# One strict load order on one queue, staged weights, and the first chunk's layers run ahead, in a fused attention and two-layer kernel

## The chip, the cores and the metric

One core of one Trainium2 chip. The metric is the device time of a whole execution in microseconds (us); lower is better. Each kernel has several executions. The ratios compare fast runs alone. The kernel before ran in every set on the same chip as the kernels that are compared with it.

## The reference

Eight batches of eight-head attention (576 positions, head size 64). The first four heads look at the last 32 positions ("local"), the other four at every 32nd ("strided"). The result, 4608 tokens of 512 features, goes through two dense layers.

```python
scores = scale * q @ k.T
scores = where(mask_local if h < 4 else mask_strided, scores, -1e9)
x = softmax(scores) @ v                  # to (4608 tokens, 512)
h = x @ w_in                             # 512 -> 2048
g = maximum(h, 0) + alpha * minimum(h, 0)
out = g @ w_out                          # 2048 -> 512
```

q, k, v and the weights arrive as float32. The kernel computes in float16.

## The kernel before

The tokens are cut into nine chunks of 512. Chunk n needs the attention of batches up to n (chunk 1 needs part of batch 1, and so on, since a batch is 576 tokens). Layer 1 of a chunk is 16 linear pieces of four matmuls of 512 columns, layer 2 the same, 0.86 us each at full clock. The attention is cut into some 30 pieces a batch: transposes of q and k ("tp"), scores ("sp") with their exp on ScalarE and mask, products with v ("pv") with their norms on DVE, transposes of the result ("xp"). The trick of the tuned kernel is to set these small pieces between linear ones, so that TensorE never waits for the other engines.

A steady loop does, for every n, layer 2 of chunk n and layer 1 of chunk n+1 beside the attention of batch n+2. What differs between the two kernels is the ramp in front of it, and the first turn (n = 1):

```python
# weights: gpsimd DMAs that cast to float16 on the way
def load_w(c, second): nc.gpsimd.dma_start(win16[...] or wout16[...], ...)
...
gate = cpool.tile([128, 16], F16)                      # SyncE waits for w_in here
nc.sync.dma_start(gate, win16[:, 0, 1008:1024])
...                                                    # then batch 1's loads
for m in range(16):                                    # layer 1, chunk 0
    lin1_piece(0, m, True)
    if m == 8: ...                                     # casts of batch 1, loads of batch 2, w_out
    attn_n(0 if m < 12 else 1, end1)
while pos["i"] < end1: attn_step(end1)                 # rest of batch 1, first pieces of batch 2
for m in range(16):                                    # layer 1, chunk 1
    lin1_piece(1, m, True)
    attn_n(0 if m < 8 else 1, end2)
for i in range(16):                                    # layer 2, chunk 0
    lin2_piece(0, i)
    attn_n(2, end2)
for n in range(1, NCH):                                # the full loop
    for i in range(16):
        lin2_piece(n, i);  attn_step(ab)
        lin1_piece(n + 1, i);  attn_step(ab)
```

The order of pieces above is the order of instructions on every engine, and a held instruction holds those behind it (in the changed kernel, scores that TensorE ends at 73.2 us get their exp at 79.05, behind an output copy that waits). Four `lin2_piece` calls end in one output copy ("osb") on ScalarE and one store on SyncE. In the traces that follow, line 437 of the kernel before is 454 of the changed one (layer 1), 482 is 499 (layer 2), 487 is 504 (output copy).

The softmax here doesn't subtract the row's maximum and nothing guards it: scores larger than these inputs give would overflow.

## Time and profile before

| | kernel before |
|---|---|
| median time | 363.43 us (363.37 to 363.66, 3 runs) |
| first linear piece | 32.2 us |
| TensorE full from | 119.1 us to the end |
| ramp: layer 1 chunk 0, layer 1 chunk 1, layer 2 chunk 0 start at | 32.2, 79.3, 97.6 us |
| one turn of the full loop | 34.5 us |

Read it so: from 119.1 us on the kernel is a steady loop with a full TensorE, and of this loop the change touches only the first turn, n = 1. All that the change can win or lose is the moment at which that loop begins. The lines that carry this are in the prediction below.

### The profile page before, as it was taken

The page shows a single profiled execution, that of the slowest core. Times are in us where ns is not written, and L with a number is a line of the kernel's source. Part 1 is how long each engine was busy: PE and PEld are TensorE (multiplying, and loading weights), DVE is VectorE, ACT ScalarE, POOL GpSimd, SP SyncE. Part 2 cuts the span into 40 slices and gives each one's busy share as a digit, 9 for nine tenths or more (in the row PEclk, how much of TensorE's full clock was granted, in tenths as well). Part 3 has the DMA queues.
Part 4 walks back from the last instruction along what each step waited for, and adds up shares of the span by engine and source line. Part 5 has one row for each costly group of instructions (what it writes and reads, how often), then busy time and mean ns, then how long its engine had stood idle before and what let it go on. Part 6 is the DMA issues. An engine that isn't in the chain of part 4 may idle for free.

```text
span 363.0 us, 6353 instructions
## 1 busy us (share of the span) xinstructions
PE 329.7 (91%) x2449; PEld 185.8 (51%) x2449; DVE 226.5 (62%) x423; ACT 177.6 (49%) x328; POOL 138.7 (38%) x170
## 2 busy tenths in 40 slices
PE   6658974649998999999999999999999999999996
PEld 3353443424564455555557776555555444444444
DVE  5776898837864477758676767585767444444410
ACT  2532663516643556565656565656554544444421
POOL 5360473381576365546455564556151000000000
PEclk9977997559999999999999999999999999999999
DMA  7989999999936083519352820000000010010012
GB/s 210 218 134 287 199 238 196 275 206 280 232 103 203 32 232 96 175 42 246 96 175 53 242 63 32 29 32 29 31 32 29 29 60 29 29 60 29 29 61 87
DMA packets 52926, 44.08 MB, mean 121 GB/s; under 512 B 33616, under 2 KB 38112, under 8 KB 52896
## 3 DMA queue, kind: packets, MB, share of 16 engines
q1 hardware_dynamic: 47712, 37.11, 38.8%
q0 software_dynamic: 4640, 5.51, 8.2%
q10 hardware_dynamic: 544, 1.05, 1.0%
q8 instruction: 19, 0.31, 0.4%
q14 instruction: 11, 0.09, 0.1%
HBM read 38.42 MB, written 9.44 MB: 132 GB/s over the span
## 4 chain that ended last, share of the span: by engine, by line
PE 81%; DMA 9%; DVE 3%; ACT 2%; POOL 2%; issue 2%; SPq 1%; POOLq 0%; ACTq 0%
PE hps L437 34%; PE ops L482 34%; DMA sttl<-in_k_dram 6%; PE sp L251 4%; PE tp L210 3%; PE pv L280 3%; DMA stv<-in_v_dram 3%; PE xp L297 2%; SPq L100 1%; PE ops L473 1%; DVE et L266 1%; DVE x L289 1%; ACT osb L487 1%; POOL vs L151 1%; ACT et L259 0%
## 5 line engine op out<-in xcount | busy, mean ns | idle before, releaser
L437 PE MATMUL hps<-xT,win 128*128 128x512 f16 (+1 forms) x640 | 148.3, 364 | 0.8 <-DVE gT L450 0.8
L450 DVE SCALAR_TENSOR_TENSOR gT<-neg,oma,hps 128x512 f16<-128x512 f32 x144 | 106.9, 743 | 59.2 <-ACT neg L447 56.7
L482 PE MATMUL ops<-wout,gT 128*128 128x512 f16 x560 | 141.4, 379 | 2.0 <-ACT osb L487 2.0
L447 ACT ACTIVATE neg<-hps 128x512 f32<-128x512 f32 x144 | 86.2, 599 | 94.9 <-PE hps L437 94.0
L266 POOL TENSOR_TENSOR et<-et,consts 128x384 f16<-128x384 f16 (+2 forms) x60 | 54.2, 908 | 85.4 <-ACT et L259 84.5
L437 PEld LDWEIGHTS <-win 128*128 128x128 f16 x640 | 60.1, 99 | 49.8 <-issue 6.0
L482 PEld LDWEIGHTS <-gT 128*128 128x128 f16 x560 | 50.4, 98 | 49.0 <-issue 2.8
L259 ACT ACTIVATE et<-sp 128x384 f16<-128x384 f32 (+2 forms) x96 | 45.6, 490 | 24.6 <-PE sp L251 24.4
L289 DVE TENSOR_TENSOR x<-pv,rc 72x384 f16<-72x384 f32 (+2 forms) x80 | 42.2, 527 | 2.7
L223 DVE COPY qpad<-tp 64x1024 f16<-64x1024 f16 x32 | 39.0, 1220 | 3.8 <-PE tp L210 3.5
L251 PE MATMUL sp<-qpad,kT 128*128 128x144 f16 (+1 forms) x224 | 32.8, 248 | 7.2 <-DVE qpad L240 3.8
L287 DVE RECIPROCAL rc<-pv 72x6 f32<-72x6 f32 (+2 forms) x80 | 14.8, 186 | 37.5 <-PE pv L280 37.3
L280 PEld LDWEIGHTS <-et 72*128 72x128 f16 (+1 forms) x448 | 25.6, 102 | 23.7 <-POOL et L262 3.7
L251 PEld LDWEIGHTS <-kT 128*128 128x128 f16 x224 | 20.5, 103 | 25.4 <-issue 5.7
L487 ACT COPY osb<-ops 128x512 f32<-128x512 f32 x35 | 20.5, 586 | 21.9 <-PE ops L482 21.9
L236 ACT COPY kT<-tp 128x1024 f16<-128x1024 f16 x16 | 16.2, 1011 | 20.0 <-PE tp L210 20.0
L280 PE MATMUL pv<-vl,et 128*128 128x65 f16 x192 | 12.4, 201 | 8.1 <-POOL et L262 3.4
L280 PE MATMUL pv<-vs,et 72*128 72x65 f16 x256 | 16.9, 200 | 1.7 <-DVE x L289 0.9
L151 POOL CAST vs<-stv 72x1024 f16<-72x1024 f32 x16 | 16.9, 1084 | 2.9 <-DMA stv<-in_v_dram 2.9
L297 PE MATMUL xp<-consts,x 72*128 72x72 f16 (+1 forms) x224 | 15.3, 211 | 2.0 <-DVE x L289 1.7
L297 PEld LDWEIGHTS <-x 72*128 72x128 f16 (+1 forms) x224 | 12.8, 104 | 7.2 <-DVE x L289 2.4
L151 POOL CAST tl<-sttl 128x512 f16<-128x512 f32 x8 | 4.9, 618 | 28.6 <-DMA sttl<-in_k_dram 28.6
(48 smaller groups left out, 186.4 us busy)
## 6 DMA issues: line engine op xcount, KB each, us to landing
out_dram<-osb SPq DMA_DIRECT2D x35, 256.0 KB, 2.0
stq<-in_q_dram SPq DMA_DIRECT2D x16, 512.0 KB, 6.7
stk<-in_k_dram SPq DMA_DIRECT2D x12, 512.0 KB, 5.0
stv<-in_v_dram SPq DMA_DIRECT2D x7, 768.0 KB
stv<-in_v_dram SPq DMA_DIRECT2D x8, 576.0 KB
win<-in_moe_w_in_dram POOLq DMA_DIRECT2D x4, 512.0 KB, 9.3
wout<-in_moe_w_out_dram POOLq DMA_DIRECT2D x4, 512.0 KB, 13.4
stk<-in_k_dram ACTq DMA_DIRECT2D x2, 512.0 KB, 8.4
```

The costliest lines, as they stand in the source:

```text
L151: keep(nc.gpsimd.tensor_copy(o, i))
L223: keep(nc.vector.tensor_copy(split(qpads[u % 2][rr, :, hh, :])[0], main[rr]))
L251: keep(nc.tensor.matmul(sp[:, 2 * w * x : 2 * w * x + 2 * w], P.kT[:, k0 : k0 + 128], P.qpad[:, :, w * t : w * t + w], start=(x == 0), sto ...
L259: keep(nc.scalar.activation(et[0:r, 0:n], sp[0:r, 0:n], AF.Exp, scale=SCALE))
L266: keep(eng.tensor_tensor(ev, ev, m.unsqueeze(1).to_broadcast([r, n // w, w]), op=ALU.mult))
L280: keep(nc.tensor.matmul(pv[:, 65 * x : 65 * x + 65], et[0:r, c : c + 128], v16[0:r, t, 2 * P.pr + hh, :], start=(x == 0), stop=(x == nb - ...
L289: keep(nc.vector.tensor_tensor(P.x16[0:w, c0 : c0 + 64 * nb].rearrange("r (c e) -> r c e", e=64), pvv[:, :, 0:64], rc[0:w, 0:nb].unsqueeze ...
L297: keep(nc.tensor.transpose(xp[:, P.w * t : P.w * t + P.w], P.x16[0 : P.w, 128 * t : 128 * t + 128], ident[0 : P.w, 0 : P.w]))
L437: keep(nc.tensor.matmul(hps[:, dst : dst + w], win16[:, kk, 128 * m : 128 * m + 128], xT[:, kk, src : src + w], start=(kk == 0 and x == 0) ...
L447: keep(nc.scalar.activation(neg, hps, AF.Relu, scale=-1.0))
L450: keep(nc.vector.scalar_tensor_tensor(gTs[n][:, m, :], neg, oma[:, m : m + 1], hps, op0=ALU.mult, op1=ALU.add))
L482: keep(nc.tensor.matmul(ops, gTs[n][:, kf, 128 * mt : 128 * mt + 128], wout16[:, kf, :], start=(kf == 0), stop=(kf == 15)))
```

## The change

The intent: TensorE idles in front because batch 1 arrives late, so order the loads by when they are needed, all on SyncE's queue: batch 0, w_in, w_out, batches 1 and 2. With w_out there early, layer 2 of chunk 0 need not come after layer 1 of chunk 1. Both layers of chunk 0 run right after batch 0's attention and cover batch 1's loads. The weights come as float32 into the v buffers and are cast on GpSimd. The core of the diff:

```diff
-    st = spool.tile([128, 2, 512], F32, tag="qk", bufs=6, ...)
+    st = spool.tile([128, 2, 512], F32, tag="qk", bufs=4, ...)
-                keep(nc.vector.tensor_copy(split(qpads[u % 2][rr, :, hh, :])[0], main[rr]))
+                copy = nc.scalar.copy if b < 3 and hh else nc.vector.tensor_copy
+                keep(copy(split(qpads[u % 2][rr, :, hh, :])[0], main[rr]))
-        eng = nc.vector if P.b < 2 else nc.gpsimd
+        eng = nc.vector if P.b < 2 and i % 2 == 0 else nc.gpsimd
...
     def load_w(c, second):
-        ... nc.gpsimd.dma_start(win16 / wout16, ...)
+        st = spool.tile([128, 2048], F32, tag="v", bufs=4, name="stw")
+        keep(nc.sync.dma_start(st.rearrange(...), w_ap(c, second)[0]))
+        staged[(c, second)] = st
+    def cast_w(c, second, eng0="pool", eng1="pool"): ...   # two copies to float16
...
+    for second in (False, True):
+        for c in range(4):
+            load_w(c, second)
+    for b in (1, 2):
+        load_qk(b, True); load_tail(b); load_v(b, True)
+        load_qk(b, False); load_v(b, False)
...
     for m in range(16):
         lin1_piece(0, m, True)
-        ...
-        attn_n(0 if m < 12 else 1, end1)
+        if m in (4, 7, 10, 13):
+            cast_w((m - 4) // 3, True, "pool", "pool" if m < 13 else "act")
+        attn_n(0, end1)
+    cast_qk(1, True, "dve", "act"); cast_tail(1, "pool"); cast_v(1, True)
+    for i in range(16):
+        lin2_piece(0, i)
+        attn_n(0 if i < 5 else 1, end1)
+        if i == 12:
+            cast_qk(1, False, "dve", "act"); cast_v(1, False)
     while pos["i"] < end1:
         attn_step(end1)
...
     for m in range(16):
         lin1_piece(1, m, True)
-        attn_n(0 if m < 8 else 1, end2)
-    for i in range(16):
-        lin2_piece(0, i)
-        attn_n(2, end2)
+        attn_n((0 if m < 2 else 1) if m < 8 else 2, end2)
     while pos["i"] < end2:
         attn_step(end2)
...
     for n in range(1, NCH):
         for i in range(16):
+            now = 0 if n == 1 and i < 3 else ab
```

Smaller parts: the attention of batches 0 to 2 becomes a sequence of its own for each batch (strided heads, then local), one more exp buffer, more v buffers.

More of the change, by code (lines that the diff above doesn't have):

```diff
@@ L82 @@
     xT = cpool.tile([128, 4, RING], F16)
-    NE = 8
+    NE = 9
     qpads = [cpool.tile([128, 2, 2, S], F16, name=f"qpad{i}") for i in range(2)]
@@ L97, in load_qk @@
         for nm, src, eng in (("q", q, nc.sync), ("k", k, k_eng or nc.sync)):
-            st = spool.tile([128, 2, 512], F32, tag="qk", bufs=6, name=f"st{nm}")
+            st = spool.tile([128, 2, 512], F32, tag="qk", bufs=4, name=f"st{nm}")
             base = src[b, h0 : h0 + 1, 0:1, :]
@@ L114, in load_v @@
     def load_v(b, strided):
-        st = spool.tile([128, 2048], F32, tag="v", name="stv")
+        st = spool.tile([128, 2048], F32, tag="v", bufs=4, name="stv")
         if strided:
@@ L324, in X, with first, sc, pv @@
         return lambda: x_piece(pairs[g])
-    feed(T(1, "q"), 0)
-    feed(T(1, "k"), 0)
-    for g in (2, 3):
-        for i in range(3):
-            feed(Sc(g, i), 0)
-    for g in (2, 3):
-        for i in range(3):
-            feed(Pv(g, i), 0)
-    feed(T(0, "q"), 0)
-    feed(T(0, "k"), 0)
-    feed(X(2), 0)
-    feed(X(3), 0)
-    for g in (0, 1):
-        for i in range(3):
-            feed(Sc(g, i), 0)
-    for g in (0, 1):
-        for i in range(2):
-            feed(Pv(g, i), 0)
-    feed(X(0), 0)
-    feed(X(1), 3)
+    def first(u0, u1):
+        A, Bp = (2 * u0, 2 * u0 + 1), (2 * u1, 2 * u1 + 1)
+        def sc(gs):
+            for g in gs:
+                for i in range(3):
+                    feed(Sc(g, i), -1)
+        def pv(gs):
+            for g in gs:
+                for i in range(len(pairs[g].pgroups)):
+                    feed(Pv(g, i), -1)
+        def tr(u):
+            feed(T(u, "q"), -1)
+            feed(T(u, "k"), -1)
+        def xs(gs, last=False):
+            for g in gs:
+                feed(X(g), g if last else -1)
+        tr(u0)
+        sc(A)
+        tr(u1)
+        sc(Bp[:1])
+        pv(A)
+        sc(Bp[1:])
+        xs(A)
+        pv(Bp)
+        xs(Bp)
+    first(1, 0)
     end0 = len(pieces)
+    first(3, 2)
+    end1 = len(pieces)
+    first(5, 4)
+    end2 = len(pieces)
     casts = []
@@ L354, in plan_casts @@
         u = (g + 3) // 2
-        if u >= 2 * B or u < 2:
+        if u >= 2 * B or u < 7:
             return []
@@ L359, in plan_casts @@
         return [(b, strided, nm, pr) for nm, pr in names]
-    for g in range(3, npair + 2):
+    for g in range(11, npair + 2):
         a, p, t, x = g, g - 1, g + 1, g - 2
-        okA = 4 <= a < npair
-        okP = 4 <= p < npair
-        okT = 4 <= t < npair and t % 2 == 0
-        okX = 4 <= x < npair
+        okA = 12 <= a < npair
+        okP = 12 <= p < npair
+        okT = 12 <= t < npair and t % 2 == 0
+        okX = 12 <= x < npair
         nP = len(pairs[p].pgroups) if okP else 0
@@ L488, in lin2_piece, with w_ap, cast_w @@
             keep(nc.sync.dma_start(out[r0 : r0 + 128, :], osb))
-    def load_w(c, second):
-        if second:
-            keep(nc.gpsimd.dma_start(
-                wout16[:, 4 * c : 4 * c + 4, :],
-                moe_w_out[512 * c : 512 * c + 512, :].rearrange("(kf p) c -> p kf c", p=128)))
-        else:
-            keep(nc.gpsimd.dma_start(
-                win16[:, :, 512 * c : 512 * c + 512],
-                moe_w_in[:, 512 * c : 512 * c + 512].rearrange("(kk p) c -> p kk c", p=128)))
+    staged = {}
+    def w_ap(c, second):
+        if second:
+            return (moe_w_out[512 * c : 512 * c + 512, :].rearrange("(kf p) c -> p kf c", p=128),
+                    wout16[:, 4 * c : 4 * c + 4, :])
+        return (moe_w_in[:, 512 * c : 512 * c + 512].rearrange("(kk p) c -> p kk c", p=128),
+                win16[:, :, 512 * c : 512 * c + 512])
+    def load_w(c, second):
+        st = spool.tile([128, 2048], F32, tag="v", bufs=4, name="stw")
+        keep(nc.sync.dma_start(st.rearrange("p (x c) -> p x c", x=4), w_ap(c, second)[0]))
+        staged[(c, second)] = st
+    def cast_w(c, second, eng0="pool", eng1="pool"):
+        s4 = staged[(c, second)].rearrange("p (x c) -> p x c", x=4)
+        dst = w_ap(c, second)[1]
+        cast_copy(eng0, dst[:, 0:2, :], s4[:, 0:2, :])
+        cast_copy(eng1, dst[:, 2:4, :], s4[:, 2:4, :])
     def warm(n):
@@ L520 @@
     load_v(0, False)
+    for second in (False, True):
+        for c in range(4):
+            load_w(c, second)
+    for b in (1, 2):
+        load_qk(b, True)
+        load_tail(b)
+        load_v(b, True)
+        load_qk(b, False)
+        load_v(b, False)
     for i in range(2):
@@ L525 @@
         keep(nc.vector.memset(kTs[i][:, :, 608:672], 0.0))
-    warm(12)
-    cast_part(0, True, "q", 0, "dve")
-    cast_part(0, True, "k", 0, "act")
-    cast_tail(0, "pool")
-    cast_part(0, True, "v", 0, "pool")
-    cast_part(0, True, "v", 1, "pool")
-    cast_part(0, False, "v", 0, "pool")
-    load_w(0, False)
-    cast_part(0, False, "v", 1, "pool")
-    load_w(1, False)
-    load_w(2, False)
-    load_w(3, False)
-    apt = pspool.tile([128, 512], F32, tag="ps", name="apt")
-    for i in range(end0):
-        if i == 8:
-            cast_part(0, False, "q", 0, "dve")
-            cast_part(0, False, "k", 0, "act")
-        attn_step(end0)
-        if i < 2:
-            warm(4)
-        elif i < 14:
-            warm(1)
-        if i == 13:
-            keep(nc.vector.tensor_copy(id16, ident[0:16, 0:16]))
-            keep(nc.tensor.transpose(apt[:, 0:16], alpha_r, id16))
-            keep(nc.vector.tensor_scalar(
-                oma, apt[:, 0:16], -1.0, 1.0, op0=ALU.mult, op1=ALU.add))
-    gate = cpool.tile([128, 16], F16)
-    keep(nc.sync.dma_start(gate, win16[:, 0, 1008:1024]))
-    for strided in (False, True):
-        load_qk(1, strided, nc.gpsimd)
-        if not strided:
-            load_tail(1)
-        load_v(1, strided)
     def attn_n(n, end):
@@ L567, in attn_n, with cast_qk, cast_v @@
             attn_step(0)
-    end1 = attn_until(1)
+    def cast_qk(b, strided, e0, e1):
+        cast_part(b, strided, "q", 0, e0)
+        cast_part(b, strided, "k", 0, e1)
+    def cast_v(b, strided, eng="pool"):
+        for pr in range(2):
+            cast_part(b, strided, "v", pr, eng)
+    warm(12)
+    cast_qk(0, True, "dve", "act")
+    cast_tail(0, "pool")
+    apt = pspool.tile([128, 512], F32, tag="ps", name="apt")
+    for i in range(end0):
+        if i == 2:
+            keep(nc.vector.tensor_copy(id16, ident[0:16, 0:16]))
+            keep(nc.tensor.transpose(apt[:, 0:16], alpha_r, id16))
+            keep(nc.vector.tensor_scalar(
+                oma, apt[:, 0:16], -1.0, 1.0, op0=ALU.mult, op1=ALU.add))
+        if i == 5:
+            cast_part(0, True, "v", 0, "pool")
+        if i == 8:
+            cast_qk(0, False, "dve", "act")
+            cast_part(0, True, "v", 1, "pool")
+        if i == 19:
+            cast_v(0, False)
+        attn_step(end0)
+        if i < 2:
+            warm(4)
+        elif i < 16:
+            warm(1)
@@ L571 @@
+    for c in range(4):
+        cast_w(c, False)
     for m in range(16):
         lin1_piece(0, m, True)
-        if m == 8:
-            cast_tail(1, "pool")
-            cast_part(1, False, "q", 0, "pool")
-            cast_part(1, False, "k", 0, "pool")
-            load_part(2, False, "qk")
-            for pr in range(2):
-                cast_part(1, False, "v", pr, "pool")
-            load_part(2, False, "v")
-            for c in range(4):
-                load_w(c, True)
-        attn_n(0 if m < 12 else 1, end1)
+        if m in (4, 7, 10, 13):
+            cast_w((m - 4) // 3, True, "pool", "pool" if m < 13 else "act")
+        attn_n(0, end1)
@@ L584 @@
+    cast_qk(1, True, "dve", "act")
+    cast_tail(1, "pool")
+    cast_v(1, True)
+    for i in range(16):
+        lin2_piece(0, i)
+        attn_n(0 if i < 5 else 1, end1)
+        if i == 12:
+            cast_qk(1, False, "dve", "act")
+            cast_v(1, False)
     while pos["i"] < end1:
         attn_step(end1)
-    end2 = attn_until(2)
+    cast_qk(2, True, "pool", "pool")
+    cast_tail(2, "pool")
+    cast_v(2, True)
+    load_qk(3, False)
+    load_tail(3)
     for m in range(16):
@@ L588 @@
         lin1_piece(1, m, True)
-        attn_n(0 if m < 8 else 1, end2)
-    for i in range(16):
-        lin2_piece(0, i)
-        attn_n(2, end2)
+        attn_n((0 if m < 2 else 1) if m < 8 else 2, end2)
+        if m == 7:
+            cast_qk(2, False, "pool", "pool")
+            cast_v(2, False)
+            load_v(3, False)
+            load_qk(3, True)
+            load_v(3, True)
     while pos["i"] < end2:
         attn_step(end2)
+    cast_tail(3, "pool")
+    cast_qk(3, False, "pool", "pool")
@@ L596 @@
+    load_part(4, False, "qk")
+    cast_v(3, False)
+    load_part(4, False, "v")
     for n in range(1, NCH):
@@ L598 @@
         for i in range(16):
+            now = 0 if n == 1 and i < 3 else ab
             lin2_piece(n, i)
-            attn_step(ab)
+            attn_step(now)
             if n + 1 < NCH:
                 lin1_piece(n + 1, i)
-                attn_step(ab)
+                attn_step(now)
         while pos["i"] < ab:
```

## The prediction

> **What bounds the kernel now.** I read the page's slices first, to see where TensorE is not full, then the busy-time table by stage, then the chain of waits in order of time, then the issue times of the SyncE queue.
>
> ```profile
> PE   6658974649998999999999999999999999999996
> ...
> PEclk9977997559999999999999999999999999999999
> DMA  7989999999936083519352820000000010010012
> ```
> A slice is 9.07 us. TensorE is full from the tenth slice to the end; what can be won lies in front. There the DMA engines are full too (7 to 9 tenths up to slice 11), and twice the clock falls to half. By stage:
>
> ```profile
> core 0: us, PE busy (x) PEld busy (x) DVE busy (x) ACT busy (x) POOL busy (x), PEclk, DMA share, GB/s
> 12.50:32.20 19.70, 13.25 (x143) 10.00 (x143) 16.14 (x41) 7.99 (x17) 8.41 (x10) 0.82 0.97 176
> 32.20:45.00 12.80, 12.79 (x52) 5.40 (x52) 8.66 (x12) 7.15 (x12) 4.05 (x5) 0.87 1.04 245
> 45.00:59.30 14.30, 8.04 (x93) 5.44 (x91) 13.38 (x23) 7.43 (x16) 7.95 (x11) 1.00 1.17 223
> 59.30:79.30 20.00, 10.32 (x113) 8.71 (x111) 12.34 (x31) 6.05 (x13) 11.05 (x12) 0.50 1.15 243
> 79.30:97.60 18.30, 17.94 (x105) 8.58 (x103) 14.73 (x24) 11.64 (x21) 7.22 (x9) 0.89 1.04 226
> 97.60:119.10 21.50, 19.52 (x178) 11.42 (x177) 12.60 (x25) 9.33 (x18) 14.43 (x16) 1.00 0.53 168
> 119.10:153.60 34.50, 34.48 (x276) 19.20 (x276) 23.12 (x45) 19.60 (x37) 18.88 (x21) 1.00 0.50 141
> ```
> The cuts are mine: attention of batch 0; layer 1 of chunk 0; two stretches of batch 1's attention; layer 1 of chunk 1; layer 2 of chunk 0; from 119.1 the full loop. TensorE loses 6.3 + 9.7 us idle between 45 and 79.3, with half clock in the second part, and 2.0 us in 97.6 to 119.1. The chain says why:
>
> ```profile
> 44.42 13.93 DMA sttl<-in_k_dram
> ...
> 65.29 9.59 DMA stv<-in_v_dram
> 74.94 2.04 POOL vs L151 x2
> ...
> 79.52 9.71 PE hps L437 x36
> ```
> Batch 1 is waited for at 44 to 58 and 65 to 75: its loads queue with batch 2's and with layer 2's weights. One more line matters, the first group of SyncE's waits that a weight gate causes:
>
> ```profile
> SPq L556 <- DMA win<-in_moe_w_in_dram: 23.4, 1, 23.4
> ```
>
> **What the Trainium skill says.** "DMA: Bandwidth & Descriptors", section "Queues, rings and completion order": on one DMA engine descriptors are consumed in ring order, and all of SyncE's transfers share one row of rings. So a small store issued behind large loads waits for them. The trace fits: the 128 KB tails of batch 1 took 11 us to land (page, DMA issues), against 2.0 us for the 256 KB stores, most of which were issued with an empty queue. Same page, "Specifications": transfers under 512 B are below line rate. The trace agrees: stretches of 2 KB rows move some 380 to 420 GB/s, stretches of 256 B rows (v of the local heads, tails) some 200. "TensorE: Matmul & The Clock Gate", "What's actually happening": the clock is half after an idle window of about 3.4 us and full after a busy one. The trace agrees: granted clock 0.50 in 59.3 to 79.3, and the first two layer 1 pieces at 32.2 took about 1.7 us each, the later ones 0.86.
>
> **The change part by part.** The built lists of instructions per engine show the new order.
>
> Weights. Eight gpsimd transfers that cast on the way go; eight SyncE loads into the v buffers (now 4) come, with 15 GpSimd casts and one on ScalarE. A 1 MB load of 2 KB rows at 390 GB/s is 2.7 us; a cast of 128x1024 on GpSimd is 1.05 us (row of q casts: 1048 ns). w_in: four loads start behind batch 0 at 17.7 us (v's cast starts 17.78), land by 31; casts 8 x 1.05 = 8.4 us from about 28. Layer 1 consumes a quarter per 4 x 0.86 us, so this hides. w_out: each load waits for the cast that frees its buffer; landed by about 43, cast by 46. Batch 1 then lands at 46 (strided) to 56 (all): q and k 4 x 1.4 us, tails 1.4, v 1.6 + 3.9. So the order does what it wants: batch 1 is no longer late.
>
> Batch 0's attention. The mask goes to GpSimd for every odd group (0.91 to 1.0 us instead of 0.37 to 0.54), and the second half of each qpad copy goes from DVE (1.22 us) to ScalarE (about 1.0). But the list shows that the ScalarE half waits for the DVE half, and kT's copy (1.01) stands behind it: 1.2 + 1.0 + 1.0 + 0.3 + 0.5 = 4.0 us from transposes to scores, where it was 2.46 + 0.5. DVE saves 2 x 1.22 + 4 masks = 4 us, and the chain gives back 1 to 2 per unit. From the second unit's first exp: masks 1.9, six norms 3.9, masks 0.75, four norms 2.8, copy 0.45 = 9.8 us. Transposes at 17.1, scores 21.8, layer 1 at about 32. It was 32.2: nothing won.
>
> Layer 1 and 2 of chunk 0. Layer 1: 2 x 1.7 + 14 x 0.86 = 15.5, to 47.5. Layer 2 starts at once: 16 x 0.86 = 13.8, plus 11 pieces of batch 1's attention at 0.15 to 0.5 us, plus 2 us for the first scores' 4 us chain, one piece of waiting for the q cast and the output copies: to about 69. At 69 the old kernel had done neither layer 2 of chunk 0 nor all of batch 1. Here the new one is ahead by 13.8 us of layer 2 less some 13 pieces (13 x 6.8/30 = 3 us; 6.8 is the 34.5 us loop less 32 pieces of 0.865): about 11 us.
>
> Then it gives back, in four places.
> (a) The fourth output copy on ScalarE needs the buffer of the first store (three buffers). SyncE issues in strict order, and that store stands behind batch 2's local q, k and v, whose first waits for batch 1's local q cast, emitted at the thirteenth piece of layer 2: about 66.5. q and k 2.8 us, v 3.9, then the store, with about 2 us of latency: lands at about 76. ScalarE, at the copy at 70.6, stands until then: 5.5 us, and batch 1's exps stand behind it.
> (b) 19 attention pieces of batch 1 run with no linear work between: 9.8 us after the first exp, while they need TensorE for 19 x 0.23 = 4.3. So layer 1 of chunk 1 begins at 86.5 (80.5 without (a)), old: 79.3.
> (c) Layer 1 of chunk 1 now carries all 30 pieces of batch 2. DVE: 16 x 0.743 = 11.9 for gT, 2 x 1.22 + 1.0 for qpad, 6.7 for norms, 0.9 for copies: 22.9. Two chains make it wait: scores of the strided unit at 9.5 us (half clock, then 4 us chain); four masks and two casts on GpSimd at 1 us each put the local unit's transposes at 16 and its scores at 20.6. After that DVE has 6 x 0.75 + 3.9 + 2.8 = 11.2 us left, and the last transposes: 33 us. The old kernel took 119.1 - 79.3 = 39.8 for this and layer 2 of chunk 0.
> (d) The loop starts at n = 1 with an empty attention pipeline: 38 pieces instead of 30, the last 12 alone: 8 x 0.23 + about 2.5 = 4.5 us.
>
> Sum with (a): 86.5 + 33 + 4.5 = 124, against 119.1: +5, 368 us. Without (a): 118, so 362.
>
> **The rivals.** First: the store does not hold ScalarE and the hand count of (c) is too long, because pieces overlap more than a count of hand-overs shows. If (c) is bound by TensorE (13.8 + 1.7 for half clock + 6.8 = 22.3) or by DVE's 22.9, it takes 24 to 26: then 80.5 + 25 + 4 = 109.5, 353.5 us. For it speaks that the old stretch 97.6 to 119.1, with 22 of the same pieces in 16 slots, took only 21.5 for 18.8 of work. Against it: there DVE had no gT to do. Second: GpSimd becomes the bound. Against it: some 20 us of work in the 33 of (c); it sets single waits, not the sum. Third: DMA stays the bound (casts late, loads starved). Then w_out lands at 48 or later and layer 2 starts 3 us later: 365 to 371. Against it: 16 MB by 56 us needs only the 380 to 420 GB/s which 2 KB rows show already. Fourth: the gain is simply the removed idle, 16 us at 45 to 79: 347. I hold it unlikely, since the same waits come back as hand-overs between DVE, ScalarE and GpSimd.
>
> **Range and chances.** Full sum 368 (weight 0.45), the sum without the held store 362 (0.3), the lean case 353.5 (0.25): mean 362.6; I say 362.0. Range 352.0 to 370.0. Faster than 356.2: 0.25; slower than 370.7: 0.16; between: 0.59.
>
> **What would show it.** The weights' order right: batch 1's tail cast waits for no DMA over 2 us, TensorE full from 32 to about 66. (a): a ScalarE wait of some 5 us on a store before the fourth output copy at about 70. (b): a stretch of about 10 us after it with DVE full and TensorE half busy, clock 0.5. (c): DVE over 65% and TensorE under 75% from the first chunk 1 piece to the first layer 2 piece of chunk 1, some 33 us; 25 would prove the lean case. (d): the loop of n = 1 at 38 to 39 us instead of 34.5; later loops 34.5 as before. I am wrong if layer 2 of chunk 1 starts before 112 us (old: 119.1), or if TensorE waits for batch 1's DMA before 69 us.

## The result, and the profile after

The changed kernel is slower: 379.44 us median (378.96 to 381.55, 4 runs) against 363.55 us (363.37 to 365.81, 4 runs) of the kernel before on the same chip. The ratio is 1.043, 95% interval 1.038 to 1.049. A ratio here and below is the mean time of one kernel's fast runs over that of the other's of the same rounds, so it is not quite the ratio of the medians quoted.

The page's slices of the changed kernel, TensorE and its granted clock (a slice is 9.4 us):

```profile
PE   6767987538777999969999999999999999999996
...
PEclk9888999955999899969999999999999999999999
```

The kernel before had 7, 4, 6 and 4 tenths in slices 6 to 9 and was full from the tenth. The changed one has 8, 7, 5 and 3 there, then 8, 7, 7 and 7 where the old one was full, and a new dip to 6 in the eighteenth slice, with the clock at 6 as well. The busy-time table by the stages of the changed kernel (cuts mine: layer 1 of chunk 0; layer 2 of chunk 0; the rest of batch 1's attention; layer 1 of chunk 1 with batch 2's attention; the loop of n = 1):

```profile
core 0: us, PE busy (x) PEld busy (x) DVE busy (x) ACT busy (x) POOL busy (x), PEclk, DMA share, GB/s
...
33.70:49.30 15.60, 15.60 (x65) 6.66 (x65) 10.89 (x15) 9.46 (x16) 10.67 (x11) 0.90 1.03 344
49.30:72.30 23.00, 17.47 (x116) 9.02 (x114) 7.54 (x12) 11.41 (x19) 6.88 (x7) 1.00 0.91 221
72.30:89.80 17.50, 8.55 (x96) 6.04 (x97) 9.84 (x27) 4.53 (x10) 6.30 (x7) 0.56 0.55 151
89.80:123.20 33.40, 25.49 (x214) 13.79 (x213) 21.80 (x44) 19.45 (x36) 17.33 (x21) 0.91 0.41 100
123.20:165.00 41.80, 38.43 (x303) 21.30 (x300) 28.02 (x52) 22.29 (x43) 25.77 (x30) 0.95 0.79 205
```

Three stages carry the loss. From 72.3 to 89.8 attention runs alone, TensorE half busy at half clock. From 89.8 to 123.2 TensorE has 25.5 us of work in 33.4, while DVE, the busiest of the others, is at 21.8: no engine is full, so it is waits that set the length. And the loop of n = 1 takes far more than the steady 34.5.

**The held store.** The chain of waits of the changed kernel, in order of time (start, duration, what):

```profile
67.65 0.61 DVE q L149
...
68.28 0.62 SPq L100
...
69.70 0.56 SPq L125
...
70.30 8.17 DMA out_dram<-osb
...
78.57 0.07 ACT osb L504
...
79.05 1.27 ACT et L260 x3
```

DVE casts batch 1's local q, which frees a buffer. Only then can SyncE issue batch 2's q (68.28), k and v (69.70), and only then the output store that stood behind them. It takes 8.2 us to land behind these loads, against a median of 2.0 for all output stores. ScalarE stands at the fourth output copy until then, and three exps stand behind it. In its list of waits:

```profile
ACT osb L504 <- DMA out_dram<-osb: 6.1, 1, 6.1
```

**Layer 1 of chunk 1.** What TensorE waited for between 89.8 and 123.2 (total, times, longest):

```profile
PE sp L252 <- DVE qpad L241: 2.5, 1, 2.5
PE sp L252 <- ACT kT L237: 1.4, 1, 1.4
PE xp L298 <- DVE x L290: 1.2, 4, 0.4
```

These are hand-overs: scores wait for the copies of q and k, transposes for the norms.

**The end of n = 1.** The attention pipeline starts empty there, so twelve pieces run behind the last linear piece, from 159.2 to 166.4. GpSimd's row of the timeline there (start, duration, engine, line, operation):

```profile
161.14 0.91 POOL L263 TENSOR_TENSOR et<-et,consts 128x384 f16<-128x384 f16 x1
161.99 2.04 POOL L151 CAST vs<-stv 72x1024 f16<-72x1024 f32 x2
163.99 1.77 POOL L267 TENSOR_TENSOR et<-et,consts 128x384 f16<-128x384 f16 x2
```

and TensorE's:

```profile
164.95 0.29 PE L281 MATMUL pv<-vl,et 128*128 128x65 f16 x2 [1.82 <-POOL et L267]
...
166.38 1.90 PE L499 MATMUL ops<-wout,gT 128*128 128x512 f16 x4
```

TensorE waits 1.8 us for a mask that stands behind two casts of the next batch's v on GpSimd. The four matmuls of the first linear piece of n = 2 then take 1.90 us, where a full-clock piece has 1.03: the clock has fallen once more.

From here on both kernels run the same loop. The first output copy of n = 2 is at 161.54 us before and at 175.95 after, 14.4 us later, and this difference stays to the last output.

### The profile page after: what moved, and what is told of

It is laid out like the page before. It is cut to its first block, busy times and chain, and to the rows that moved or that the text cites. A ratio compares the mean times of both kernels' runs of the same rounds, so it can differ in the third digit from the quotient of the medians.

```text
span 377.3 us, 6358 instructions
## 1 busy us (share of the span) xinstructions
PE 336.6 (89%) x2451; PEld 185.1 (49%) x2451; DVE 218.8 (58%) x411; ACT 185.9 (49%) x337; POOL 151.0 (40%) x180
## 4 chain that ended last, share of the span: by engine, by line
PE 72%; DVE 10%; DMA 9%; ACT 5%; issue 1%; SPq 1%; POOL 1%; ACTq 0%
PE ops L499 31%; PE hps L454 29%; DVE x L290 4%; DMA stk<-in_k_dram 4%; PE sp L252 3%; PE tp L210 3%; PE pv L281 2%; DMA out_dram<-osb 2%; DMA consts<-consts 2%; DVE et L267 2%; PE xp L298 2%; ACT kT L237 2%; DMA stv<-in_v_dram 1%; ACT et L260 1%; DVE gT L467 1%
## 5 line engine op out<-in xcount | busy, mean ns | idle before, releaser
L454 PE MATMUL hps<-xT,win 128*128 128x512 f16 (+1 forms) x640 | 150.7, 367 | 0.1
L499 PE MATMUL ops<-wout,gT 128*128 128x512 f16 x560 | 142.9, 382 | 1.5 <-ACT osb L504 1.5
L267 POOL TENSOR_TENSOR et<-et,consts 72x432 f16<-72x432 f16 (+2 forms) x68 | 62.7, 928 | 102.5 <-ACT et L260 101.6
L499 PEld LDWEIGHTS <-gT 128*128 128x128 f16 x560 | 51.2, 98 | 49.6 <-issue 3.0
L260 ACT ACTIVATE et<-sp 128x384 f16<-128x384 f32 (+2 forms) x96 | 45.2, 489 | 23.6 <-PE sp L252 23.3
L252 PE MATMUL sp<-qpad,kT 128*128 128x144 f16 (+1 forms) x224 | 31.7, 239 | 10.9 <-ACT kT L237 4.9
L224 DVE COPY qpad<-tp 64x1024 f16<-64x1024 f16 x26 | 31.7, 1219 | 11.4 <-PE tp L210 11.2
L281 PEld LDWEIGHTS <-et 72*128 72x128 f16 (+1 forms) x448 | 24.2, 103 | 23.1 <-issue 8.2
L252 PEld LDWEIGHTS <-kT 128*128 128x128 f16 x224 | 19.5, 99 | 31.1 <-ACT kT L237 6.2
L241 DVE COPY qpad<-tt 64x128 f16<-64x128 f16 x32 | 8.2, 256 | 20.7 <-ACT kT L238 20.3
L263 POOL TENSOR_TENSOR et<-et,consts 128x384 f16<-128x384 f16 x12 | 10.9, 910 | 19.1 <-ACT et L260 19.1
## 6 DMA issues: line engine op xcount, KB each, us to landing
stw<-in_moe_w_in_dram SPq DMA_DIRECT2D x4, 1024.0 KB, 10.5
```

The lines of the kernel that those rows point to most:

```text
L224: keep(copy(split(qpads[u % 2][rr, :, hh, :])[0], main[rr]))
L252: keep(nc.tensor.matmul(sp[:, 2 * w * x : 2 * w * x + 2 * w], P.kT[:, k0 : k0 + 128], P.qpad[:, :, w * t : w * t + w], start=(x == 0), sto ...
L260: keep(nc.scalar.activation(et[0:r, 0:n], sp[0:r, 0:n], AF.Exp, scale=SCALE))
L267: keep(eng.tensor_tensor(ev, ev, m.unsqueeze(1).to_broadcast([r, n // w, w]), op=ALU.mult))
L281: keep(nc.tensor.matmul(pv[:, 65 * x : 65 * x + 65], et[0:r, c : c + 128], v16[0:r, t, 2 * P.pr + hh, :], start=(x == 0), stop=(x == nb - ...
L454: keep(nc.tensor.matmul(hps[:, dst : dst + w], win16[:, kk, 128 * m : 128 * m + 128], xT[:, kk, src : src + w], start=(kk == 0 and x == 0) ...
```

## The experiments

Twelve kernels ran, in three sets, each beside the kernel before on the same chip. All gave correct results.

| kernel | median us | ratio to before | 95% interval |
|---|---|---|---|
| changed kernel | 379.44 | 1.043 | 1.038 to 1.049 |
| e1: four output buffers | 373.46 | 1.025 | 1.021 to 1.029 |
| e2: q copies back on DVE | 375.38 | 1.031 | 1.027 to 1.035 |
| e3: masks back on DVE | 379.26 | 1.041 | 1.036 to 1.046 |
| e4: weights by casting gpsimd DMAs | 383.14 | 1.050 | 1.044 to 1.056 |
| e5: e1 and e2 | 368.56 | 1.018 | 1.013 to 1.023 |
| e6: e5, attention spread over the slots | 356.79 | 0.986 | 0.979 to 0.993 |
| e7: e5, layer 2 of chunk 0 late again | 376.94 | 1.040 | 1.035 to 1.045 |
| e8: before, layer 2 of chunk 0 early | 351.75 | 0.970 | 0.965 to 0.974 |
| e9: n = 1 fed from its first slot | 375.43 | 1.034 | 1.027 to 1.041 |
| e10: the late v casts on ScalarE | 380.07 | 1.046 | 1.039 to 1.054 |
| e11: dummy matmuls in lone stretches | 375.24 | 1.033 | 1.024 to 1.042 |
| e12: e8 with four output buffers | 347.65 | 0.957 | 0.951 to 0.964 |

Without its slow run e4 has a median of 382.90. In the third set (e9 to e12) the fast runs of the kernel before spread from 361.28 to 365.63 us, so the intervals are wider. A second caution: layer 1 of chunk 0 starts between 32.6 and 35.4 us in the traces of e9, e10, e11 and the changed kernel, which are alike up to there. The ramp's first transfers vary by that much. Where two traces are compared below, I count from a common point behind it.

**e1: is it the store that holds ScalarE?**

```diff
-    opool = ctx.enter_context(tc.tile_pool(name="op", bufs=3))
+    opool = ctx.enter_context(tc.tile_pool(name="op", bufs=4))
```

> The changed kernel with four output buffers instead of three, so that the fourth output copy on ScalarE does not need the first store to have landed. Theory (order of the stores behind the loads): the 6.1 us wait of ScalarE on the store goes, layer 1 of chunk 1 starts at about 84 instead of 89.8 us, and all later stages move with it: 373 us (371 to 375) against 379.4. Rival (the wait is hidden, because batch 1's attention waits for its own chain or for batch 2 anyway): 378 to 380.

373.46 us: as expected. Layer 1 of chunk 1 starts at 82.98 instead of 89.82 us, or 34.1 instead of 40.7 us behind the start of layer 2 of chunk 0, and ScalarE's wait for a store is gone from its list. The held store costs some 6 us, all of it on the path.

**e2: is it the q copies on two engines?**

```diff
-                copy = nc.scalar.copy if b < 3 and hh else nc.vector.tensor_copy
-                keep(copy(split(qpads[u % 2][rr, :, hh, :])[0], main[rr]))
+                keep(nc.vector.tensor_copy(split(qpads[u % 2][rr, :, hh, :])[0], main[rr]))
```

> The changed kernel with both halves of the qpad copy on DVE again. Theory (the ScalarE half stands behind the DVE half and in front of kT's copy, so the split makes the path to the scores longer): each of six units gains about 1 us where TensorE stands at its first scores, in all 2 to 5 us: 375 to 377. Rival (DVE is what bounds these stages, the split takes 6 x 1.2 us off it): 382 to 386.

375.38 us: as expected, some 4 us better than the changed kernel. The line of ScalarE's waits that it removes, in the changed kernel between 50 and 72 us:

```profile
ACT qpad L224 <- DVE qpad L224: 6.1, 2, 3.7
```

The two halves were meant to be copied at once. The built program makes ScalarE's half wait for DVE's, so the split only adds a hand-over, and puts k's copy behind it. (The 3.7 us also hold the wait for the transposes: DVE's half runs from 56.16 to 57.38, ScalarE's from 57.41.)

The Trainium skill, "PSUM — Partial Sum Buffer", section "PSUM bank collisions raise a hardware error", says that two engines on one bank collide only within the same 32-partition quadrant. The halves here are partitions 0 to 63 and 64 to 127, so by the page they would not collide. The trace shows only that the program ordered them; no run here shows what a simultaneous read would do.

**e3: is it the masks?**

```diff
-        eng = nc.vector if P.b < 2 and i % 2 == 0 else nc.gpsimd
+        eng = nc.vector if P.b < 2 else nc.gpsimd
```

> The changed kernel with all masks of batches 0 and 1 on DVE again. Theory: no mask on GpSimd ends a long wait in batches 0 and 1 (its longest there is under 1 us), DVE takes 4 x 0.4 us more per batch: 379 to 382. Rival (the slow GpSimd masks delay the first units): 374 to 377.

379.26 us: no effect, as expected. Masks on GpSimd are slower, but for batches 0 and 1 they were not what the next step waited for last.

**e4: is it the staging of the weights?** The weights come by the casting gpsimd DMAs again, in the new order, w_in issued during batch 0's attention and w_out right behind; the 16 casts go.

```diff
-        st = spool.tile([128, 2048], F32, tag="v", bufs=4, name="stw")
-        keep(nc.sync.dma_start(...)); staged[(c, second)] = st
+        src, dst = w_ap(c, second)
+        keep(nc.gpsimd.dma_start(dst, src))
```

> The changed kernel with the eight weight loads as GpSimd transfers that cast on the way, as in the kernel before: no staging, no casts, and SyncE's batch 1 loads no longer stand behind the weights. Theory (weights and their casts are hidden, TensorE was fed in layer 1 of chunk 0; only batch 1's k, which came at 52 us, is late by 2 us): within 4 us of the changed kernel, 375 to 381, unless layer 1 of chunk 0 is now late because w_in shares the DMA engines with batch 1. Rival (staging and SyncE's strict order are what made the kernel slower): at or below the kernel before, 355 to 366.

383.14 us: a miss by 2 us over the expected range, and the rival (355 to 366) is refuted. The staging is not the loss; without it the kernel is no faster (383.14 against 379.44 by the medians, with intervals that overlap). That batch 1's k is cast at 49.8 instead of 52.2 us brings no gain beside this. The chain of waits of e4 shows the new wait:

```profile
30.64 22.86 DMA wout<-in_moe_w_out_dram
...
53.55 1.04 PE ops L499 x4
```

w_out now competes with batch 1's loads, which no longer stand behind it on one queue, and layer 2 of chunk 0 waits for it. The strict order does what it was meant to do for w_out.

**e5: do the two repairs add up?** e1 and e2 together.

> Four output buffers and both qpad halves on DVE together. If the wait on the store and the longer copy chain are separate losses, their gains add: 379.4 - 6.5 - 4 = 369 (367 to 371). If both stood in the same wait, no better than the first alone, 373.

368.56 us: they add. The ratio falls from 1.043 to 1.018, the sum of the two single steps (0.019 and 0.012) within the intervals. Two small details of the change are worth 9 us by the ratios, 11 by the medians, and what remains is still slower than before by 1.8%.

**e6: is what remains a matter of where the attention pieces stand?** e5 with batch 1's pieces set two or three to a slot in the second half of layer 2 of chunk 0, batch 2's likewise in layer 1 of chunk 1 with earlier casts, pv before the local scores from batch 1 on, and n = 1 fed from its first slot.

```diff
-        attn_n(0 if i < 5 else 1, end1)
+        attn_n((0, 0, 0, 0, 0, 2, 0, 0, 3, 3, 2, 2, 2, 2, 3, 3)[i], end1)
...
-        attn_n((0 if m < 2 else 1) if m < 8 else 2, end2)
+        attn_n((0, 0, 2, 0, 0, 3, 3, 2, 1, 1, 2, 2, 3, 3, 2, 2)[m], end2)
...
-            now = 0 if n == 1 and i < 3 else ab
+            now = ab
```

> The same, and batch 1's and batch 2's attention no longer run as blocks: some two pieces in each slot of layer 2 of chunk 0 and of layer 1 of chunk 1, with the casts of the local units earlier, all norms of the strided unit ahead of the local scores, and the loop of n = 1 fed from its first slot. Theory (what is lost is attention without linear work beside it, and a linear layer with more attention than DVE can follow): 8 to 14 us less than the run with both edits, 355 to 361. Rival (data come too late for it, DMA is the bound): within 3 us of that run.

356.79 us: as expected, 11.8 us better than e5 and 1.4% faster than the kernel before. The edit is a bundle: the places of the pieces, the earlier casts, the order inside a batch and e9's edit are not told apart. The time between the last output copy of n = 1 and the first of n = 2 is 11.1 us here, 18.0 in the changed kernel and 8.5 before.

**e7: does layer 2 of chunk 0 ahead of batch 1 win anything?** e5 with layer 2 of chunk 0 put back behind layer 1 of chunk 1.

```diff
-    for i in range(16):
-        lin2_piece(0, i)
-        attn_n(0 if i < 5 else 1, end1)
-    ...
     for m in range(16):
         lin1_piece(1, m, True)
-        attn_n((0 if m < 2 else 1) if m < 8 else 2, end2)
+        attn_n(0 if m < 8 else 1, end2)
+    ...
+    for i in range(16):
+        lin2_piece(0, i)
+        attn_n(2, end2)
```

> Both edits, but layer 2 of chunk 0 back behind layer 1 of chunk 1, as in the kernel before; loads, staging and casts stay as changed. Theory: batch 1's attention then waits for its data and itself with nothing beside it (layer 1 of chunk 0 ends at 49, batch 1 is all there at about 62), but batch 2 has two linear layers to hide behind again: the two balance within 6 us, 364 to 374. Rival (running both layers of chunk 0 ahead is what costs): at or under the kernel before, 355 to 364. Other rival (it is worth its full 13.8 us): 378 or more.

376.94 us: a miss, slower than my theory allowed (364 to 374). Running the layer ahead is worth 8.4 us within this order of loads. So the central idea of the change pays in this order, and the loss comes in spite of it.

**e8: the same idea in the kernel before.** The old kernel, with its casting weight DMAs and its gate, but w_out loaded right behind w_in, batch 1's k on SyncE, layer 2 of chunk 0 beside batch 1's attention and layer 1 of chunk 1 beside batch 2's, two pieces to a slot, in the old pipelined order of pieces.

```diff
     load_w(3, False)
+    for c in range(4):
+        load_w(c, True)
...
-        load_qk(1, strided, nc.gpsimd)
+        load_qk(1, strided)
...
         attn_n(0 if m < 12 else 1, end1)
+    for i in range(16):
+        lin2_piece(0, i)
+        attn_n(2, end1)
     while pos["i"] < end1:
         attn_step(end1)
     for m in range(16):
         lin1_piece(1, m, True)
-        attn_n(0 if m < 8 else 1, end2)
-    for i in range(16):
-        lin2_piece(0, i)
         attn_n(2, end2)
```

> The kernel before with one idea of the change alone: layer 2's weights loaded right behind layer 1's (still GpSimd transfers that cast, batch 1's k moved to SyncE), and layer 2 of chunk 0 run beside batch 1's attention, two pieces a slot, in the old pipelined order of pieces. Theory (the idea is sound, its blocks are not): layer 2 fills the old wait for batch 1, layer 1 of chunk 1 carries batch 2 in pipelined order: 345 to 357. Rival (any order that puts layer 2 of chunk 0 first overloads layer 1 of chunk 1): 363 to 375.

351.75 us, 3% faster than the kernel before: as expected. The first output copy of n = 2 comes at 149.23 us, 12.3 earlier than before.

**e9: what does the empty start of n = 1 cost?** The changed kernel with one edit.

```diff
-            now = 0 if n == 1 and i < 3 else ab
+            now = ab
```

> The changed kernel with one edit: in the loop of n = 1 the attention pieces start in the first slot instead of the fourth, so 32 of the 38 pieces lie beside linear pieces and 6 instead of 12 run alone behind the last one. In the trace of the changed kernel the 12 lone pieces take 7.2 us (159.15 to 166.4) for 2.8 us of TensorE work, and the first two linear pieces of n = 2 run at half clock (+1.65 us). Theory (the loop's loss is the lone tail): six pieces fewer in the tail give 3.6 us less there and cost 6 x 0.23 = 1.4 us beside linear work; with the half clock unchanged the gain is 2 to 3 us: 376 to 378. Rival (the empty start of the pipeline is what costs, because the first scores must wait for the chain of copies wherever it stands): within 1 us of the changed kernel, 378.5 to 380.5.

375.43 us: the rival is out, and the gain, 4.0 us by the medians (3.4 by the ratios), is a little over the theory's 2 to 3. The reason is the clock. TensorE at the end of n = 1 in e9:

```profile
164.66 0.23 PE L281 MATMUL pv<-vl,et 128*128 128x65 f16 x2 [0.26 <-POOL et L267]
...
165.97 1.03 PE L499 MATMUL ops<-wout,gT 128*128 128x512 f16 x4
```

With a shorter tail the wait for the mask is 0.26 instead of 1.82 us, and the first linear piece of n = 2 takes 1.03 instead of 1.90. The theory had left the half clock in place. From the first output copy of n = 1 to the first of n = 2 it is 37.6 us here against 45.3; 3.1 us of this is given back, since the first output of n = 1 comes later (55.2 instead of 52.1 us behind the last output copy of chunk 0).

**e10: what holds the mask?** The chain of waits of the changed kernel has a step from a v transfer, issued at 158.9 behind an output store, to the mask at 164.0. I had first read it as the cause. But the casts at 162.0 read an earlier load, issued at 133.6. So the edit moves the two casts to ScalarE:

```diff
-                    cast_part(b, strided, nm, pr, "pool")
+                    cast_part(b, strided, nm, pr, "act" if (b, strided, nm) == (4, True, "v") else "pool")
```

> The changed kernel with one edit: the two casts of batch 4's strided v go from GpSimd to ScalarE. In the changed kernel they stand on GpSimd at 162.0 to 164.0, in the middle of the lone tail of n = 1, ahead of two masks, and TensorE waits 1.8 us for the second mask. Theory (GpSimd's queue holds the masks): the wait goes, the tail gets 1.5 to 2 us shorter, and if the shorter idle window keeps the clock full, the 1.65 us of half clock behind it go too: 375.7 to 378. Rival (what holds the masks is a v transfer behind a store, as the chain of waits names it): no change, 379 to 380; and the line of the chain stays.

380.07 us: no gain, and the theory's 375.7 to 378 is missed. The step from the v transfer is gone from the chain nevertheless, so the rival doesn't hold either. The chain of e10 says what took its place:

```profile
163.15 0.53 ACT vs L147
...
164.10 0.49 ACT et L260
...
164.66 0.92 POOL et L267
```

The cast now stands ahead of the exp on ScalarE instead of ahead of the mask on GpSimd. TensorE's wait for the mask is 1.45 us instead of 1.82. Changing their engine inside the lone tail does not help; moving them out of it was not tried by itself.

**e11: what does the half clock cost?** The changed kernel with a dummy matmul of 512 columns behind each lone piece of batch 1, of batch 2 and of n = 1.

```diff
+    def warm2():
+        wp2 = popool.tile([128, 512], F32, tag="ops", name="wp2")
+        keep(nc.tensor.matmul(wp2, wrm[:, 0:128], wrm, start=True, stop=True))
...
         attn_step(end1)
+        warm2()
... (the same behind end2, and in n = 1)
```

> The changed kernel with one dummy matmul of 512 columns behind each attention piece that runs alone (behind layer 2 of chunk 0, behind layer 1 of chunk 1 and behind the loop of n = 1), to keep TensorE's clock up there. Theory (half clock behind the lone stretches costs 1.2 to 1.7 us at each of three places, the dummies fill only idle time): 375 to 378, and the first linear pieces behind each stretch take 0.86 instead of 1.7 us. Rival (the dummies do not fill the windows, since TensorE stands at a wait and not at a dummy, and they delay the pieces by their own 0.2 to 0.4 us): 380 to 386, clock as before.

375.24 us: as the theory had it. TensorE at the end of n = 1 in e11:

```profile
164.25 0.38 PE L537 MATMUL wp<-wrm 128*128 128x512 f16 x1
164.69 1.02 PE L499 MATMUL ops<-wout,gT 128*128 128x512 f16 x4
```

The first piece of n = 2 takes 1.02 us, and so does the first of layer 2 of chunk 1 (1.91 without dummies). Counted from the start of layer 2 of chunk 0 to the first output of n = 2 the gain is 2.7 us (124.1 against 126.8). The medians give 4.2; layer 1 of chunk 0 also started 1.1 us earlier in this trace, which is within the spread of the ramp. So the half clock behind the lone stretches is some 3 to 4 us of the loss.

The prediction quoted an idle window of about 3.4 us from the skill. Here the longest single idle of TensorE in the lone tail is 1.82 us, and the clock fell all the same. Nearer to it is a later section of the same page, "TensorE: Matmul & The Clock Gate", "A second HAM failure mode: psum-queue depth-cycling": frequent short idles between groups of matmuls make the clock swing too. No run here shows which share of idle time is enough.

**e12: the best version.** e8 with the fourth output buffer of e1.

> The best version so far (the kernel before, with layer 2's weights loaded right behind layer 1's, layer 2 of chunk 0 beside batch 1's attention and layer 1 of chunk 1 beside batch 2's; 351.75 us) with four output buffers instead of three. In its trace the first four output copies stand at 58.97 to 81.15, inside the stretch in which SyncE still issues batch 2's loads. Theory of the held store: the fourth copy waits for the first store there as well, so a fourth buffer gives 1 to 5 us: 347 to 351. Rival (in this order the first store has landed by the fourth copy, 22 us later): no change, 351 to 352.5.

347.65 us, 4.3% faster than the kernel before: as expected. In e8 ScalarE waits 4.4 us for a store at the fourth output copy, here not at all; from the start of layer 2 of chunk 0 to that copy it is 23.3 instead of 27.1 us. The busy-time table of e12 (layer 2 of chunk 0 with batch 1; layer 1 of chunk 1 with batch 2; the loop of n = 1):

```profile
core 0: us, PE busy (x) PEld busy (x) DVE busy (x) ACT busy (x) POOL busy (x), PEclk, DMA share, GB/s
...
54.40:78.00 23.60, 21.77 (x216) 13.46 (x215) 19.43 (x45) 11.66 (x24) 13.69 (x16) 1.00 1.13 253
78.00:103.00 25.00, 22.80 (x233) 14.10 (x234) 23.92 (x47) 18.76 (x37) 21.65 (x25) 1.00 1.02 257
103.00:137.00 34.00, 34.00 (x275) 19.11 (x274) 26.00 (x49) 19.79 (x38) 20.11 (x23) 1.00 0.73 184
```

Layer 1 of chunk 1 with one batch's worth of attention pieces (batch 2's, and the first of batch 3) takes 25 us where the changed kernel takes 33.4, and DVE is nearly full (23.9 of 25.0). No long stretch of attention alone is left, and the clock is full in all three stretches.

## Why the prediction was wrong

It said 362.0 us, 352 to 370, and the kernel took 379.44. The four losses (a) to (d) all came, and its own full sum (368) had the sign of the result. Three things made the number wrong: the choice between its sums (6 us), the size of (d) (5.8 us) and the start of layer 1 of chunk 1 (3.3 us). Some 2 us of the 17.4 are left, within the spread of the runs. I compare the steps in the profiled execution:

| step | predicted | measured |
|---|---|---|
| layer 1 of chunk 0 starts | 32 | 33.7 |
| layer 2 of chunk 0 starts | 47.5 | 49.1 |
| layer 1 of chunk 1 starts, with (a) and (b) | 86.5 | 89.8 |
| (c) layer 1 of chunk 1 | 33 | 33.4 |
| (d) n = 1 beyond a steady turn | 4.5 | 10.3 |
| loop start, in terms of before's 119.1 | 124 | 133.5 |

(The last line is the sum of the two above it and the start of layer 1 of chunk 1. 10.3 is the 14.4 us by which n = 2 comes late, less the 4.1 by which n = 1 starts late, 123.2 against 119.1.)

**The held store and the lean case were weighed wrongly.** 362.0 is the prediction's sum without (a), and its two cases without a held store had 0.55 of the weight. The store did hold ScalarE, for 6.1 us, and e1 shows that this lies on the path. The lean case for (c) had 0.25: layer 1 of chunk 1 was to take 33 us by the hand count or 24 to 26 by the lean one, and "25 would prove the lean case". It took 33.4, with TensorE at 25.5 us of work and DVE at 21.8, under full. The hand count of hand-overs was right. The lean case is not impossible, only not in this order of pieces: e12 carries a batch's worth in 25 us.

**(d) was mis-sized: 10.3 instead of 4.5 us.** The working was eight more pieces and 2.5 us for the lone end. Measured from the timeline: the 32 linear pieces with 26 attention pieces took 35.8 us (123.4 to 159.2), where the prediction's rates give 34.5 - 4 x 0.23 = 33.6. 1.2 of the difference is half clock in the first two linear pieces (1.71 and 1.23 instead of 0.86 each) and 0.4 the wait for the first copies; the rest I cannot place. The twelve lone pieces took 7.2 us instead of 12 x 0.23 + 2.5 = 5.3. The half clock behind them cost 1.7 us in the first two linear pieces of n = 2. Together 2.2 + 1.9 + 1.7 = 5.8, which is the gap. e9, with half of the lone pieces, wins 4 us, and e11 shows the part of the clock.

**The start: 3.3 us.** Layer 1 of chunk 1 begins 3.3 us later than predicted. 1.7 of it is there at the first linear piece; since four traces with a like front spread by 2.8 us there, part of that is chance. Another 1.7 comes between layer 2 of chunk 0 and layer 1 of chunk 1: batch 1 was to land at 46 (strided), but the first transfer that ScalarE waited for landed at 52.2:

```profile
38.42 13.77 DMA stk<-in_k_dram
```

The prediction's rate was right while data moved, but the DMA engines stood nearly still in between (GB/s is the last number of a line):

```profile
31.00:33.50 2.50, 1.08 (x12) 0.65 (x13) 2.40 (x8) 0.00 (x0) 2.50 (x4) 1.00 0.15 42
...
38.00:47.00 9.00, 9.00 (x44) 4.05 (x43) 7.85 (x11) 6.23 (x11) 5.33 (x6) 1.00 1.05 393
```

Each load of w_out waits for the casts of w_in that free its buffer: SyncE issued them from 31.43 to 37.34 us, the last landed at 47.7 (predicted: about 43), and batch 1 stands behind them. So TensorE waited for no DMA of batch 1 before 69 us only in the letter: ScalarE's cast waited 2.1 us for k, the first output copy stood behind the cast, and TensorE waited 1.0 us for that copy at 53.8. Another of its signs failed outright: GpSimd's cast of batch 1's tails was to wait for no DMA over 2 us and waited 5.5. The third rival, late DMA, was a part of the truth.

**The premise.** The prediction reads the kernel before as waiting for batch 1 from 44 to 58 and from 65 to 75 us. The two transfers that it names from the chain are, by the order of the program, batch 2's: the tails issued at 44.42, cast at 58.50, and the v issued at 65.29, cast at 74.94. (Its 11 us for batch 1's tails is the median of seven batches; batch 1's own k tail took some 10.5.) Batch 1's own casts are all done by 52.2 us. The longest waits of TensorE between 45 and 79.4 are these, and none in its list there is for a DMA or a cast:

```profile
PE sp L251 <- DVE qpad L240: 3.8, 1, 3.8
PE pv L280 <- POOL et L262: 3.4, 1, 3.4
PE pv L280 <- POOL et L266: 3.1, 1, 3.1
```

The first is a copy on DVE, which was busy for 3.7 of the 3.8 us. The other two are masks of batch 2's first pieces, which stand on GpSimd behind casts of batch 2; one of these waited 2.1 us for its load. By these waits, bringing batch 1 forward could win little, and the change did not do it: the first unit's k is cast by 43.5 us before and by 53.3 after, the strided v by 52.2 and 60.1. What pays, in e7 and e8, is filling the idle time, whatever its cause.

What held: the order of weights hides them in layer 1 (TensorE is full from 33.7 to 52.7, though not to the 66 of the prediction). (a) is a held store of 6.1 us where 5.5 was predicted, and e1 confirms its place on the path. (b) is 10.8 us from the first exp to layer 1 of chunk 1, with the clock at 0.56, where 9.8 was predicted. The later loops are as before. And layer 2 of chunk 1 started at 123.2, past the 112 that was set as the mark for being wrong. What remains without (a) and the q copies goes with e6's bundle, mostly a new placing of pieces; e9 alone is worth 3 to 4 us in the changed kernel. How much of e6 belongs to layer 2 of chunk 0, to layer 1 of chunk 1 and to the casts was not taken apart. e7's miss also stays open in its size: I can show that the early layer wins 8.4 us, not why it wins more than my count.

## What to carry to other kernels

Moving large work forward to cover a wait can leave small dependent work behind it alone, so spread the small work over the large in the same step. Here the spreading (e6, a bundle) was worth 11.8 us and two details (e5) 9 to 11, which together took the changed kernel from 4% slower to 1.4% faster; the old order of pieces with the same idea (e8, e12) is 3 to 4% faster. When a queue carries loads and stores in strict order, count the store buffers again; one more was worth 4 to 6 us in both versions. Before you move loads, see whose data a transfer in the chain of waits is, and whether the engine that idles waits for it. And where a prediction has two branches, see which one the waits of the stage support instead of averaging them.

## What the Trainium skill lacked or had wrong

- "TensorE: Matmul & The Clock Gate" ties the half clock to an idle window of about 3.4 us in its main rule. Here the longest idle was 1.82 us, in 7.2 us with TensorE busy for 4.2, and the next linear piece took 1.90 us instead of 1.03. Its later section on micro-idles is nearer, but has no number for how much idle is enough.
- "DMA: Bandwidth & Descriptors" gives the order of a ring, but no figure for a small store behind large loads. Here a 256 KB store behind about 1.8 MB of loads took 8.2 us to land against a median of 2.0, and 12.3 us in e8.
- No page that I read says that a copy out of PSUM, split by partitions over DVE and ScalarE, can come out serialized in the built program. Here it did: ScalarE's half began at 57.41 us, when DVE's half of 1.22 us had ended; taking the split back won 4 us.
- None has the caution that a step of the chain of waits can name a transfer that the waiting instruction does not use: the v transfer of 5.07 us in front of the mask at 164.0 was named so, while the cast ahead of the mask read a load issued 28 us before.
